# Fewer, larger transfers around attention: whole weight tiles on ScalarE's queue, keys and values of both batches per transfer

## The chip, the cores and the metric

One Trainium2 chip, one core of it. The metric is the device time of one execution in microseconds, the median of the runs. A smaller time is better.

## The reference

Three layers follow one another on fp32 data. With B=2, H=8 heads, S=768, D=40:

```python
# 1. mLSTM attention, per batch and head, for t in range(S):
m_new = max(f[t] + m, i[t]);  fs = exp(f[t] + m - m_new);  is_ = exp(i[t] - m_new)
C = fs * C + is_ * outer(v[t], k[t]);  n = fs * n + is_ * k[t]
y[t] = sigmoid(o[t]) * (C @ q[t]) / max(|n . q[t]|, 1)

# 2. soft mixture of 8 experts, 4 slots each, on x = y as [1536, 320]
logits = x @ phi                                  # [1536, 32]
slot_in = softmax(logits, axis=0).T @ x           # [32, 320]
slot_out[e] = relu(slot_in[e] @ w1[e]) @ w2[e]    # w1 [8,320,1024], w2 [8,1024,320]
x = softmax(logits, axis=1) @ slot_out            # [1536, 320]

# 3. domain mixture of 4 experts
out = sum_e p[:, e] * (relu(x @ u1[e]) @ u2[e])   # u1 [4,320,1024], u2 [4,1024,320]
```

In fp32, w1 and w2 are 10.5 MB each (8 x 320 x 1024 x 4 bytes), and q, k, v and o 1.97 MB each.

## The kernel before

Attention works on chunks of 128 positions: 6 chunks c in 2 batches b make 12 steps i (b = i % 2, c = i // 2). Within a step the scores of a chunk (stage_S, matmuls of L350), its decay matrix (stage_E: matmuls L300, exponentials L303 on ScalarE), the weighted values (stage_P1, L374), the state (stage_V, L422) and the transposes of keys (stage_K, L317), queries (qT, L274) and finished rows (stage_T1, L455) are spread over the engines. The loop `for i in range(2, NT - 1)` at L797 writes out the order of steps 2 to 10 by hand, and that written order is the order on each engine (`tc.manual_schedule()`). The logits of the soft mixture, `x @ phi`, start inside the loop: first in step 6 (L475).

After the loop come the experts of layer 2 (ffn1 with w1, matmuls L1127; ffn2 with w2, L1163), then layer 3 from about 116 us (L1232, L1276, L1292).

All data comes by DMA on two queues. SP's queue issues q, k, v, o, phi, probs, w2, u1 and u2. ScalarE's own instruction stream issues w1: `load_w1` at L84, called by `act_w` (L95) behind stage_E of each step, so that a w1 issue that has to wait holds back whatever ScalarE does next. A w1 tile is [128, 5, 512] (1280 KB: two experts, half of the hidden columns). It is fetched as two transfers, rows 0:2 (512 KB) and 2:5 (768 KB), and the table NW says how many of those 16 transfers a step issues: one ahead of the loop, one in step 2, two each in steps 3 to 9.

k and v of a chunk come per batch: 128 partitions x 8 heads x 40 floats, that is 160 KB in runs of 160 bytes; so do o and the first q. They lie in 3 buffers kvb (chunk c in c % 3), and a load into one waits for the readers of the chunk that lay there before. q of later chunks comes in pieces of 320 KB through two buffers qb.

Each DMA takes the next of 8 completion semaphores in turn, in the order in which the program issues DMAs on both queues. Before it is issued it waits until the DMA that took this semaphore last, 8 DMAs earlier, has landed. In the listings of instruction order below this is `[waits DMAHWn]`.

The lines that matter below: L88 (the w1 issue on ScalarE), L666 (stage gates2, exponentials EL and ER for chunks 4 and 5, in step 6), L684 (tokC, which empties the PSUM bank that L455 of step 6 then fills), L331 (sigmoid of o), L202, L209, L224 (loads of k, v, o), L103 (w2).

Of the kernel before, what the change touches and what calls it, by code (L numbers as in the profile page):

```python
# [8 lines left out]
F32 = mybir.dt.float32  # L9
# [6 lines left out]
NBIG = 11  # L16
NW3 = 5
NW = (1, 1, 2, 2, 2, 2, 2, 2, 2, 0)
WN = (2, 4, 2, 4)
# [3 lines left out]
def tile_mlstm_soft_moe_domain_moe(  # L23
# [16 lines left out]
    nc = tc.nc  # L40
    B, H, S, D = q.shape
# [17 lines left out]
    def bc(i):  # L59
        return i % B, i // B  # L60
# [4 lines left out]
    def slot(shape, name, dt=F32):  # L65
        return big.tile(shape, dt, tag="w", name=name)
# [16 lines left out]

    def load_w1(n, r0, r1):  # L84
        half, j = divmod(n, 4)
        if r0 == 0:
            w1s[half, j] = slot([128, 5, FH], f"w1_{n}")
        nc.scalar.dma_start(  # L88
            out=w1s[half, j][:, r0:r1],
            in_=w1[2 * j:2 * j + 2, :, half * FH:half * FH + FH].rearrange("e (p r) f -> (e p) r f", r=5)[:, r0:r1],  # L90
        )

    w1q = [(n, r0, r1) for n in range(8) for r0, r1 in ((0, 2), (2, 5))]

    def act_w(k=1):  # L95
        for _ in range(k):
            if w1q:
                load_w1(*w1q.pop(0))

    def load_w2(e, u, get):  # L100
        if u == 0:
            w2s[e] = get([128, 2, R2, DM], f"w2_{e}")
        nc.sync.dma_start(out=w2s[e][:, u], in_=w2[e, u * FH:(u + 1) * FH].rearrange("(p r) d -> p r d", r=R2))  # L103
# [13 lines left out]
    wq = [(e, u) for e in (0, 2, 4, 6) for u in range(2)]  # L117
    wq += [(e, u) for e0 in (1, 5) for u in range(2) for e in (e0, e0 + 2)]

# [6 lines left out]
    with tc.manual_schedule():  # L126
# [10 lines left out]
        with ExitStack() as actx:  # L137
# [83 lines left out]

            def load_o(i):
                b, c = bc(i)
                nc.sync.dma_start(  # L224
                    out=x1[b][:, c, 0:DM].rearrange("p (h d) -> p h d", d=D),
                    in_=o_gate[b, :, c * L:(c + 1) * L, :].rearrange("h p d -> p h d"),
                )

# [324 lines left out]

            os = list(range(NT))

            def load_os(n=1):
                for _ in range(n):
                    if os:
                        load_o(os.pop(0))

            nc.scalar.dma_start(out=gin[:, 1], in_=i_gate.rearrange("b h s -> (b h) s"))
# [18 lines left out]

# [437 lines left out]
        with mctx:  # L1018
# [368 lines left out]
```

## Time and profile before

| what | value |
| --- | --- |
| median of 3 runs | 325.69 us (325.62, 325.69, 328.19) |
| profiled execution, its own time | 323.16 us |
| its span, first to last instruction | 321.1 us |
| mean granted TensorE clock | 0.983 |
| TensorE busy (matmul) | 307.5 us, 96% of the span |
| VectorE, ScalarE, GpSimd busy | 167.2, 117.8, 92.6 us |
| DMA | 43.47 MB in 65133 packets, 49424 of them under 512 B |

The profiled execution is 2.53 us below the median of the runs, and 2.06 us of its time lie outside the span. TensorE's row in the page has one weak stretch: of its 40 slices (8.03 us each) the sixth is at 2 tenths. The clock row shows 6 and 7 tenths in the sixth to eighth slices and 9 elsewhere. The DMA row is at 8 or 9 up to the ninth slice, falls to 4, and is at 9 again up to the fourteenth. From about 121 us to the end TensorE works on layer 3 without a gap worth naming.

### The profile page before, as it was taken

The numbers are of one execution on the slowest core, as the hardware profiler recorded it, in microseconds if no ns is written. First come the engines' busy times: TensorE is split into PE (matmuls) and PEld (weight loads), VectorE is DVE, ScalarE is ACT, GpSimd is POOL, SyncE is SP. The second block draws the span as 40 slices with busy tenths as digits, with TensorE's granted clock in tenths as the row PEclk, the third lists the DMA queues.
The fourth block names the chain that finished last, engine by engine and source line by source line (L and its number), as shares of the span: only waits on it lengthen the run. The fifth ranks groups of instructions, "written<-read, shape, count | busy, mean of one in ns | idle before, by whom it ended". The sixth has DMA issues, their size and how long they took to land.

```text
span 321.1 us, 6916 instructions
## 1 busy us (share of the span) xinstructions
PE 307.5 (96%) x2846; PEld 271.3 (84%) x2846; DVE 167.2 (52%) x351; ACT 117.8 (37%) x259; POOL 92.6 (29%) x148
## 2 busy tenths in 40 slices
PE   8999992999999999999999999999999999999995
PEld 8878882888763448899999998999998999999995
DVE  6898993469536134564444444444444444444411
ACT  3868853666321034332222233333322222222200
POOL 8647772457422057900005600003800000000000
PEclk9999996699999999999999999999999999999999
DMA  7999999984999994129000001370001100011111
GB/s 138 197 188 307 306 290 211 291 235 166 353 416 415 352 302 131 24 65 306 2 3 0 0 2 33 100 262 2 0 0 27 41 2 0 22 41 41 43 61 41
DMA packets 65133, 43.47 MB, mean 135 GB/s; under 512 B 49424, under 2 KB 56624, under 8 KB 65104
## 3 DMA queue, kind: packets, MB, share of 16 engines
q1 hardware_dynamic: 59632, 32.50, 36.7%
q10 hardware_dynamic: 5472, 10.55, 9.7%
q8 instruction: 22, 0.36, 0.5%
q14 instruction: 7, 0.06, 0.0%
HBM read 39.50 MB, written 1.97 MB: 129 GB/s over the span
## 4 chain that ended last, share of the span: by engine, by line
PE 72%; DVE 1%; ACT 1%; issue 0%; POOL 0%; ACTq 0%
PE po L1292 53%; PE pa L1276 7%; PE ph L1127 3%; PE po L1163 3%; PE pg L1232 2%; PE kvp L990 1%; PE s L997 1%; PE pt L1035 1%; PE pt L1120 0%; PE pt L1090 0%; PE pt L1176 0%; DVE x L441 0%; PE po L1263 0%; PE pt L455 0%; POOL x L447 0%
## 5 line engine op out<-in xcount | busy, mean ns | idle before, releaser
L1292 PE MATMUL po<-uh,hh 128*128 128x320 f32 x768 | 170.3, 309 | 0.6 <-ACT hh L1281 0.6
L1292 PEld LDWEIGHTS po<-uh,hh 128*128 128x128 f32 x768 | 131.7, 188 | 5.8 <-POOL ul L1219 1.0
L1292 PE MATMUL po<-ul,hh 128*128 128x320 f32 x384 | 118.2, 309 | 0.0
L1282 DVE SCALAR_TENSOR_TENSOR hh<-pa,hh 128x512 fp32r<-128x512 f32 x96 | 65.8, 691 | 95.5 <-ACT hh L1281 95.5
L1281 ACT ACTIVATE hh<-pa 128x512 fp32r<-128x512 f32 x96 | 56.7, 599 | 121.7 <-PE pa L1276 120.5
L1292 PEld LDWEIGHTS po<-ul,hh 128*128 128x128 f32 x384 | 72.0, 188 | 0.0
L1217 POOL TENSOR_SCALAR uh<-u 128x640 fp32r<-128x640 f32 x16 | 11.6, 727 | 90.6 <-PE po L1292 76.3
L1276 PE MATMUL pa<-cS,gs 128*128 128x512 f32 x96 | 37.0, 397 | 0.2 <-ACT gs L1270 0.2
L1219 POOL TENSOR_TENSOR ul<-u,uh 128x640 fp32r<-128x640 f32 x16 | 25.1, 1569 | 1.3
L1300 DVE SCALAR_TENSOR_TENSOR acc<-po,pr,acc 128x320 f32<-128x320 f32 x36 | 19.6, 543 | 10.6 <-PE po L1292 10.6
L1276 PEld LDWEIGHTS pa<-cS,gs 128*128 128x128 f32 x96 | 17.9, 188 | 1.2 <-issue 0.4
L309 POOL TENSOR_SCALAR_AFFINE_SELECT w<-w 128x512 f32<-128x512 f32 x24 | 14.8, 641 | 6.4 <-ACT w L303 6.4
L356 DVE TENSOR_TENSOR w<-w,pss 128x512 f32<-128x512 f32 x24 | 15.4, 681 | 2.2 <-PE pss L350 2.0
L303 ACT ACTIVATE w<-pt 128x512 f32<-128x512 f32 x24 | 13.0, 595 | 5.6 <-PE pt L300 3.2
L350 PE MATMUL pss<-qT,kT 64*128 64x128 f32 x192 | 15.0, 299 | 0.0
L350 PEld LDWEIGHTS pss<-qT,kT 64*128 64x128 f32 x192 | 12.6, 198 | 1.8 <-issue 0.6
L447 POOL TENSOR_TENSOR x<-x,rd 128x320 f32<-128x320 f32 x11 | 8.8, 798 | 15.2 <-DVE rd L404 15.2
L455 PE MATMUL pt<-ident,x 128*128 128x128 f32 x36 | 6.5, 295 | 6.7 <-issue 6.1
L374 PE MATMUL p<-kvb,w 128*64 128x64 f32 x320 | 11.7, 230 | 0.0
L374 PEld LDWEIGHTS p<-kvb,w 128*64 128x64 f32 x320 | 11.0, 146 | 0.2 <-issue 0.2
L455 PEld LDWEIGHTS pt<-ident,x 128*128 128x128 f32 x36 | 4.1, 147 | 8.0 <-issue 6.6
L1163 PE MATMUL po<-w,hT 128*32 128x320 f32 x128 | 9.2, 434 | 0.0
(250 smaller groups left out, 316.4 us busy)
## 6 DMA issues: line engine op xcount, KB each, us to landing
w<-in_moe_w_dram SPq DMA_DIRECT2D x16, 640.0 KB, 9.1
w<-in_moe_w_dram ACTq DMA_DIRECT2D x8, 768.0 KB, 6.5
w<-in_moe_w_dram ACTq DMA_DIRECT2D x8, 512.0 KB, 4.5
u1a<-in_moe_w_dram SPq DMA_DIRECT2D x4, 1024.0 KB, 8.9
u<-in_moe_w_dram SPq DMA_DIRECT2D x3, 1280.0 KB, 10.6
kvb<-in_k_dram SPq DMA_DIRECT2D x12, 160.0 KB, 4.5
kvb<-in_v_dram SPq DMA_DIRECT2D x12, 160.0 KB, 5.3
x<-in_o_gate_dram SPq DMA_DIRECT2D x12, 160.0 KB, 4.9
```

The lines of the kernel that those rows point to most:

```text
L303: nc.scalar.activation(out=w.rearrange("p g t -> p (g t)"), in_=pt, func=AF.Exp)
L309: nc.gpsimd.affine_select(out=w, in_=w, compare_op=ALU.is_ge, fill=0.0, base=0, pattern=[[0, HP], [1, L]], channel_multiplier=-1)
L350: nc.tensor.matmul(out=pss[j][:, g, :], lhsT=kT[i][64 * j:64 * j + 64, g, :], rhs=q_of(i)[64 * j:64 * j + 64, g, :], start=True, stop=True)
L356: nc.vector.tensor_tensor(out=w, in0=w, in1=pS.pop((i, j)), op=ALU.mult)
L374: nc.tensor.matmul(out=p1[64 * x:64 * x + 64, h, :], lhsT=W[i, h % 2][:, h // 2, 64 * x:64 * x + 64], rhs=vb(i)[:, h, :], start=True, stop ...
L1163: nc.tensor.matmul(out=pos[hf][32 * j:32 * j + 32, 0:DM], lhsT=hT[:, r, 32 * j:32 * j + 32], rhs=w2s[2 * j + hf][:, r // R2, r % R2, :], s ...
L1219: nc.gpsimd.tensor_tensor(out=lo[:, r0:r0 + 2], in0=raw[:, r0:r0 + 2], in1=hi[:, r0:r0 + 2].bitcast(F32), op=ALU.subtract)
L1276: nc.tensor.matmul(out=pa, lhsT=GS[e][0][:, ft * 128:(ft + 1) * 128], rhs=cS[:, tg * 512:(tg + 1) * 512], start=True, stop=True)
L1281: nc.scalar.activation(out=hi, in_=pa, func=AF.Relu)
L1282: nc.vector.scalar_tensor_tensor(out=lo, in0=pa, scalar=0.0, in1=hi.bitcast(F32), op0=ALU.max, op1=ALU.subtract)
L1292: nc.tensor.matmul(out=po[:, 0:DM], lhsT=x[:, sl], rhs=y[e][:, ft, :], start=(ft == 0 and n == 0), stop=(ft == FT - 1 and n == 2))
L1300: nc.vector.scalar_tensor_tensor(out=dst, in0=po[:, 0:DM], scalar=pr[:, i, e:e + 1], in1=dst, op0=ALU.mult, op1=ALU.add)
```

## The change

- w1 goes as 8 transfers of 1280 KB in place of 16. The new table issues one behind stage_E of steps 2, 4, 6, 7, 8, 9 and 10, and the last behind the loop.
- k (from chunk 1 on) and v go as one transfer of 320 KB for both batches, 128 partitions x 16 x 40, so 11 transfers in place of 22. Where they stand in the program is set by a new table SPQ, together with o (four at a time, both batches of two chunks), q and phi. phi moves from step 3 to step 5, behind q7.
- Ahead of the loop SP issues what the list `k1 q2 v0 o0 q3 o1 v1 k2 q4 v2 q5` says.
- Two of the three kvb buffers, now called kw, belong to the pool that stays, with the q buffer behind each; w2 of experts 0 and 2 is loaded into them from step 9 on, half by half. The order of w2 becomes 0, 2, 4, 6, 7, 1, then 3 and 5 by halves, and NW3 (buffers of a later pool) becomes 3.

```diff
-NW3 = 5
-NW = (1, 1, 2, 2, 2, 2, 2, 2, 2, 0)
+NW3 = 3
+SPQ = {2: "k3 o2", 3: "v3 o3", 4: "k4 q6", 5: "v4 q7 p", 6: "k5 o4", 7: "o5", 8: "v5", 9: "d w"}
+NW = {2: 1, 4: 1, 6: 1, 7: 1, 8: 1, 9: 1, 10: 1}
...
-    def load_w1(n, r0, r1):
+    def load_w1(n):
         half, j = divmod(n, 4)
-        if r0 == 0:
-            w1s[half, j] = slot([128, 5, FH], f"w1_{n}")
+        w1s[half, j] = slot([128, 5, FH], f"w1_{n}")
         nc.scalar.dma_start(
-            out=w1s[half, j][:, r0:r1],
-            in_=w1[2 * j:2 * j + 2, :, half * FH:half * FH + FH].rearrange("e (p r) f -> (e p) r f", r=5)[:, r0:r1],
+            out=w1s[half, j],
+            in_=w1[2 * j:2 * j + 2, :, half * FH:half * FH + FH].rearrange("e (p r) f -> (e p) r f", r=5),
         )
...
     wq = [(e, u) for e in (0, 2, 4, 6) for u in range(2)]
-    wq += [(e, u) for e0 in (1, 5) for u in range(2) for e in (e0, e0 + 2)]
+    wq += [(e, u) for e in (7, 1) for u in range(2)]
+    wq += [(e, u) for u in range(2) for e in (3, 5)]
...
-            kvb = [ap.tile([128, 2, B, H, 64], F32, name=f"kvb{i}") for i in range(NB)]
+            KVN = 2 * B * H * 64
+            kw = [tp.tile([128, KVN + 2 * DM], F32, name=f"kw{i}") for i in range(2)]
+            kvb = [t[:, 0:KVN].rearrange("p (x b h d) -> p x b h d", x=2, b=B, h=H) for t in kw]
+            kvb.append(ap.tile([128, 2, B, H, 64], F32, name="kvb2"))
+            qw = [t[:, KVN:].rearrange("p (h x) -> p h x", h=H) for t in kw]
+            for e in (0, 2):
+                w2s[e] = kw[e // 2][:, 0:2 * R2 * DM].rearrange("p (u r d) -> p u r d", u=2, r=R2)
...
-            def load_v(i):
-                b, c = bc(i)
+            def load_kv(x, c):
+                src = (k, v)[x]
                 nc.sync.dma_start(
-                    out=vb(i)[:, :, 0:D],
-                    in_=v[b, :, c * L:(c + 1) * L, :].rearrange("h p d -> p h d"),
+                    out=kvb[c % NB][:, x].rearrange("p b h d -> p (b h) d")[:, :, 0:D],
+                    in_=src[:, :, c * L:(c + 1) * L, :].rearrange("b h p d -> p (b h) d"),
                 )
...
-            load_k(2)
-            load_q(2)
-            load_v(0)
-            load_os()
-            load_v(1)
-            load_k(3)
-            load_q(3)
-            load_os()
-            load_v(2)
-            load_q(4)
-            load_v(3)
+            load_set("k1 q2 v0 o0 q3 o1 v1 k2 q4 v2 q5")
...
-            load_k(4)
-            load_os()
-            act_w(NW[0])
-            load_q(5)
             stage_Wk(2)
             stage_T2(1)
...
                 stage_S(i)
-                if i + 3 < NT:
-                    load_k(i + 3)
-                if i in (4, 5):
-                    load_q(i + 2)
-                load_os(2 if i in (5, 6) else 1)
-                if i + 2 < NT:
-                    load_v(i + 2)
-                if i == 3:
-                    nc.sync.dma_start(out=phi_sb[:, 0:2, :], in_=phi[0:256].rearrange("(k p) n -> p k n", p=128))
-                    nc.sync.dma_start(out=phi_sb[0:64, 2, :], in_=phi[256:320])
+                load_set(SPQ.get(i, ""))
                 stage_W(i, 0)
                 stage_E(i + 1)
-                act_w(NW[i - 1])
+                act_w(NW.get(i, 0))
                 stage_P2(i)
...
             stage_T2(iL)
+            load_w(2)
+            act_w()
             stage_P1(iL - 1, "kv")
...
-            load_w(8, slot3)
+            load_w(6, slot3)
```

Before, ScalarE in step 6: w are the exponentials of the decay matrix, EL and ER those of the gates, x1_1 rows of o.

```order
L460 ACTIVATE xT_844<-pt_827 128x384 [waits PE_49]
L303 ACTIVATE w_863<-pt_861 128x512 [waits PE_49]
L303 ACTIVATE w_867<-pt_865 128x512 [waits PE_49]
L88 DMA w1_4_869<-in_moe_w1_dram 128x2x512 [waits DMAHW6_49,Pool_49]
L88 DMA w1_4_869<-in_moe_w1_dram 128x3x512 [waits DMAHW1_49]
L666 ACTIVATE EL_90<-gt2_95,gs0_92 128x256 [waits DVE_49]
```

The last DMAs on these two semaphores are the k load of chunk 4, batch 1 (DMAHW6) and the second o load (DMAHW1) of the listing of SP below. After the change, the same place:

```order
L486 ACTIVATE xT_826<-pt_809 128x384 [waits PE_49]
L329 ACTIVATE w_844<-pt_842 128x512 [waits PE_49]
L329 ACTIVATE w_848<-pt_846 128x512 [waits PE_49]
L88 DMA w1_2_850<-in_moe_w1_dram 128x5x512 [waits DMAHW0_49]
L675 ACTIVATE EL_90<-gt2_95,gs0_92 128x256 [waits DVE_49]
```

One issue stands where two stood, and its semaphore was last taken by q7, the load of kw1 from q in the second listing of SP below. Before, SP's queue in steps 5 and 6 (kvb are keys and values, x1 the o gate):

```order
L209 DMA kvb0_85<-in_v_dram 128x8x40 [waits DMAHW4_49,PE_49]
L202 DMA kvb1_86<-in_k_dram 128x8x40 [waits DMAHW6_49,PE_49,Pool_49]
L224 DMA x1_0_97<-in_o_gate_dram 128x8x40 [waits DMAHW7_49]
L224 DMA x1_1_98<-in_o_gate_dram 128x8x40 [waits DMAHW1_49]
L209 DMA kvb1_86<-in_v_dram 128x8x40 [waits DMAHW2_49,PE_49]
L202 DMA kvb2_87<-in_k_dram 128x8x40 [waits DMAHW3_49,Pool_49]
```

After the change, SP's queue in steps 4 to 6:

```order
L216 DMA kw1_86<-in_k_dram 128x16x40 [waits DMAHW4_49,PE_49,Pool_49]
L204 DMA kw0_85<-in_q_dram 128x8x80 [waits DMAHW5_49,Activation_49]
L216 DMA kw1_86<-in_v_dram 128x16x40 [waits DMAHW7_49,DMAHW0_49,PE_49]
L204 DMA kw1_86<-in_q_dram 128x8x80 [waits DMAHW0_49,Activation_49]
L239 DMA phi_sb_64<-in_moe_phi_dram 128x2x32 [waits DMAHW1_49]
L240 DMA phi_sb_64<-in_moe_phi_dram 64x32 [waits DMAHW2_49]
L216 DMA kvb2_87<-in_k_dram 128x16x40 [waits DMAHW3_49,Pool_49]
```

q7 itself waits on DMAHW0, which the first w1 tile took, and phi now stands right behind it; before, phi stood in step 3. Behind the loop SP's queue holds, after the change, w2 of experts 0 and 2 in kw:

```order
L102 DMA kw0_85<-in_moe_w2_dram 128x1280 [waits DMAHW5_49,PE_49,Pool_49]
L102 DMA kw0_85<-in_moe_w2_dram 128x1280 [waits DMAHW7_49,PE_49,Activation_49]
L102 DMA kw1_86<-in_moe_w2_dram 128x1280 [waits DMAHW1_49,PE_49,Pool_49]
L102 DMA kw1_86<-in_moe_w2_dram 128x1280 [waits DMAHW0_49,DMAHW3_49,PE_49,Activation_49]
L102 DMA w2_4_1487<-in_moe_w2_dram 128x1280 [waits DVE_49,DMAHW5_49,PE_49,Activation_49]
```

Before, the same place of SP's queue reads:

```order
L103 DMA w2_0_1506<-in_moe_w2_dram 128x1280 [waits DMAHW4_49,PE_49,Activation_49]
L103 DMA w2_0_1506<-in_moe_w2_dram 128x1280 [waits DMAHW5_49]
L103 DMA w2_2_1509<-in_moe_w2_dram 128x1280 [waits DMAHW6_49,DVE_49,Pool_49]
L103 DMA w2_2_1509<-in_moe_w2_dram 128x1280 [waits DMAHW7_49]
L103 DMA w2_4_1512<-in_moe_w2_dram 128x1280 [waits DMAHW2_49,DMAHW3_49,DMAHW0_49,PE_49]
```

There the first of them was issued at 79.61 us, in step 11. Now the halves of w2_0 wait for the last readers of chunk 3 (steps 6 and 7), and those of w2_2 for the last readers of chunk 4 (steps 8 and 9). The order of the instructions on TensorE (1113 rows) and VectorE (265 rows) is the same in both kernels.

## Rows read from the trace of the kernel before

**Rows 1.** The page: rows of TensorE and its clock, 40 slices.

```profile
PE   8999992999999999999999999999999999999995
...
PEclk9999996699999999999999999999999999999999
```

**Rows 2.** Windows, of steps 2, 6, 7 and 9, then of layer 2's ffn.

```profile
core 0: us, PE busy (x) PEld busy (x) DVE busy (x) ACT busy (x) POOL busy (x), PEclk, DMA share, GB/s
18.51:26.41 7.90, 7.11 (x116) 5.67 (x115) 6.38 (x15) 4.29 (x13) 4.16 (x7) 1.00 1.06 226
...
43.17:55.74 12.57, 6.51 (x119) 5.46 (x118) 6.60 (x18) 5.15 (x16) 5.55 (x8) 0.81 1.01 252
55.74:63.87 8.13, 8.13 (x100) 7.12 (x99) 3.99 (x11) 4.69 (x13) 3.33 (x5) 0.67 1.13 289
...
70.11:74.70 4.59, 4.59 (x90) 4.01 (x90) 3.86 (x12) 2.77 (x8) 2.63 (x4) 1.00 0.45 135
...
94.60:104.50 9.90, 9.90 (x91) 3.30 (x94) 5.58 (x18) 1.35 (x4) 2.08 (x2) 1.00 1.02 415
```

**Rows 3.** Timeline of TensorE: start, us, engine, line, operation, count, idle before it.

```profile
16.08 1.15 PE L374 MATMUL p<-kvb,w 128*64 128x64 f32 x32
...
23.59 0.66 PE L274 MATMUL pt<-ident,qb 128*128 128x128 f32 x4 [0.79 <-ACT w L303]
...
43.17 1.16 PE L350 MATMUL pss<-qT,kT 64*128 64x128 f32 x16
...
46.24 0.62 PE L422 MATMUL kv<-kvb,wkb 128*64 128x41 f32 x16
...
47.16 0.86 PE L475 MATMUL pt<-xT,phi_sb 128*32 128x128 f32 x24
...
54.67 0.87 PE L455 MATMUL pt<-ident,x 128*128 128x128 f32 x3 [6.06 <-issue]
...
55.74 2.08 PE L350 MATMUL pss<-qT,kT 64*128 64x128 f32 x16
...
61.23 0.61 PE L422 MATMUL kv<-kvb,wkb 128*64 128x41 f32 x16
```

**Rows 4.** Timeline of ScalarE in steps 2 and 6; ACTq are its DMA issues.

```profile
20.12 0.46 ACT L331 ACTIVATE x<-x 128x320 f32<-128x320 f32 x1
22.43 0.46 ACTq L88 DMA_DIRECT2D w<-in_moe_w_dram  x1
22.93 1.08 ACT L303 ACTIVATE w<-pt 128x512 f32<-128x512 f32 x2 [2.35 <-PE pt L317]
...
34.73 0.90 ACTq L88 DMA_DIRECT2D w<-in_moe_w_dram  x2
...
46.05 1.08 ACT L303 ACTIVATE w<-pt 128x512 f32<-128x512 f32 x2
51.12 2.15 ACTq L88 DMA_DIRECT2D w<-in_moe_w_dram  x2
53.31 0.60 ACT L666 ACTIVATE EL<-gt,gs 128x256 fp32r<-128x256 f32 x1 [6.18 <-DMA x<-in_o_gate_dram]
```

**Rows 5.** Timeline of SP's queue: start and length of single issues.

```profile
31.78 3.87 SPq L209 DMA_DIRECT2D kvb<-in_v_dram  x1
...
44.10 4.37 SPq L202 DMA_DIRECT2D kvb<-in_k_dram  x1
```

**Rows 6.** DMA issues of SP starting at 3.91, 17.83, 44.10 and 100.40: KB, us to landing.

```profile
kvb<-in_k_dram SPq DMA_DIRECT2D x1, 160.0 KB, 3.8
...
kvb<-in_k_dram SPq DMA_DIRECT2D x1, 160.0 KB, 3.6
...
kvb<-in_k_dram SPq DMA_DIRECT2D x1, 160.0 KB, 6.9
...
w<-in_moe_w_dram SPq DMA_DIRECT2D x1, 640.0 KB, 9.0
```

**Rows 7.** Timeline of TensorE: the second batch of ffn2 matmuls.

```profile
107.41 5.59 PE L1163 MATMUL po<-w,hT 128*32 128x320 f32 x80
```

More of the change, by code (lines that the diff above doesn't have):

```diff
@@ L82, in tile_mlstm_soft_moe_domain_moe @@
     u2s = {}
-    def load_w1(n, r0, r1):
+    def load_w1(n):
         half, j = divmod(n, 4)
-        if r0 == 0:
-            w1s[half, j] = slot([128, 5, FH], f"w1_{n}")
+        w1s[half, j] = slot([128, 5, FH], f"w1_{n}")
         nc.scalar.dma_start(
-            out=w1s[half, j][:, r0:r1],
-            in_=w1[2 * j:2 * j + 2, :, half * FH:half * FH + FH].rearrange("e (p r) f -> (e p) r f", r=5)[:, r0:r1],
+            out=w1s[half, j],
+            in_=w1[2 * j:2 * j + 2, :, half * FH:half * FH + FH].rearrange("e (p r) f -> (e p) r f", r=5),
         )
-    w1q = [(n, r0, r1) for n in range(8) for r0, r1 in ((0, 2), (2, 5))]
+    w1q = list(range(8))
     def act_w(k=1):
         for _ in range(k):
-            if w1q:
-                load_w1(*w1q.pop(0))
+            load_w1(w1q.pop(0))
     def load_w2(e, u, get):
-        if u == 0:
+        if u == 0 and e not in w2s:
             w2s[e] = get([128, 2, R2, DM], f"w2_{e}")
@@ L142, in tile_mlstm_soft_moe_domain_moe @@
             NB = 3
-            kvb = [ap.tile([128, 2, B, H, 64], F32, name=f"kvb{i}") for i in range(NB)]
+            OP = 0
+            KVN = 2 * B * H * 64
[5 more added lines that the diff above has]
+                w2s[e] = kw[e // 2][:, 0:2 * R2 * DM].rearrange("p (u r d) -> p u r d", u=2, r=R2)
             wkb = [ap.tile([128, H, 64], F32, name=f"wkb{i}") for i in range(2)]
@@ L195, in load_q @@
                 else:
-                    qb[n] = ap.tile([128, H, 2 * D], F32, tag="qb", bufs=2, name="qb")
+                    qb[n] = qw[n % 2]
                     nc.sync.dma_start(out=qb[n].rearrange("p h x -> p (h x)")[:, 0:H * r * D].rearrange("p (h x) -> p h x", h=H),
@@ L220, in x1_of, with load_o, load_phi, load_probs @@
                 return x1[b][:, c]
[L222 to L227, printed above, removed]
+            def load_o(n):
+                c, b = divmod(n, B)
+                for x in (2 * c, 2 * c + 1) if not OP else (2 * c,):
+                    y = x + 1 + OP
+                    nc.sync.dma_start(
+                        out=x1[b][:, x:y, 0:DM].rearrange("p c (h d) -> p c h d", d=D),
+                        in_=o_gate[b, :, x * L:y * L, :].rearrange("h (c p) d -> p c h d", p=L),
+                    )
+            def load_phi():
+                nc.sync.dma_start(out=phi_sb[:, 0:2, :], in_=phi[0:256].rearrange("(k p) n -> p k n", p=128))
+                nc.sync.dma_start(out=phi_sb[0:64, 2, :], in_=phi[256:320])
+            def load_probs():
+                for b in range(B):
+                    nc.sync.dma_start(out=pr[:, b::B, :], in_=probs[b * S:(b + 1) * S].rearrange("(c p) e -> p c e", p=128))
+            def load_set(names):
+                for x in names.split():
+                    if x[0] in "kv":
+                        load_kv("kv".index(x[0]), int(x[1:]))
+                    elif x[0] in "oq":
+                        (load_o if x[0] == "o" else load_q)(int(x[1:]))
+                    else:
+                        {"p": load_phi, "d": load_probs, "w": lambda: load_w(2)}[x]()
             for n in range(4):
@@ L552, in fill @@
                     nc.tensor.matmul(out=FB[:, 0:128], lhsT=x, rhs=x, start=True, stop=True)
[L554 to L559, printed above, removed]
             nc.scalar.dma_start(out=gin[:, 1], in_=i_gate.rearrange("b h s -> (b h) s"))
@@ L1025, in slot3 @@
                 return mp.tile(shape, dt, tag="w3", bufs=NW3, name=name)
-            for b in range(B):
-                nc.sync.dma_start(out=pr[:, b::B, :], in_=probs[b * S:(b + 1) * S].rearrange("(c p) e -> p c e", p=128))
-            load_w(8, slot3)
+            load_w(6, slot3)
             cps = {}
```

## The prediction

> **What bounds the kernel now.** I read the page first, then a window for each step, then the timelines of the engines in the weak step, and last the DMA issues. In the page TensorE's row is at 9 tenths almost everywhere, so the kernel is bound by TensorE, and only a hole in that row can be won by moving loads [rows 1]. There is one large hole, in the sixth slice, and the granted clock is down in the same slices. The windows put it in step 6: 12.57 us long with 6.51 us of matmuls at a mean clock of 0.81; step 7 behind it is busy all its 8.13 us, but at 0.67 [rows 2]. TensorE's timeline shows it as one gap: idle 6.06 us ahead of L455 at 54.67 [rows 3]. The profile names no releaser for it, so I followed the data: L455 needs the PSUM bank that tokC on ScalarE empties, and tokC stands behind EL (L666). ScalarE ends its exponentials at 47.13 (46.05 + 1.08), and then its w1 issues take until 53.27; EL waits 6.18 us [rows 4]. The two issues of w1_4 wait for the k load of chunk 4 (issued at 44.10, landed 6.9 us later, at 51.0 [rows 5, 6]) and for the o load behind it. So the hole is a weight load, needed 40 us later, that sits in ScalarE's stream ahead of urgent work.
>
> A smaller hole of the same kind is in step 2: the first w1 issue goes out at 22.43, the exponentials follow at 22.93, and TensorE idles 0.79 us for them [rows 3, 4].
>
> **The change, term by term** (against the profiled execution of 323.16 us, which lies 2.53 below the median).
>
> *Step 6, the idle time.* Of 16 issues 8 remain, one here, and it waits for q7. If q7 has landed when ScalarE comes to it, the issue costs what an issue that waits for nothing costs: 0.46 in step 2, 0.90 for two in step 4 [rows 4]; I take 0.4. When does q7 land? A 160 KB transfer takes 0.86 us of the queue: from the k load of 3.91 (landing 3.8 later) to that of 17.83 (landing 3.6 later) there are 16 such units, in 13.7 us [rows 6]. A w1 tile is 1280 KB, 3.16 us at the 415 GB/s of the ffn window [rows 2]. Queued up to q5 are 24 units, so q5 lands at about 3.9 + 23 x 0.86 = 23.8. Behind it, up to q7, come 16 units and 2 w1 tiles, 20.1 us: 43.9. Between the landings of the k loads of 17.83 and 44.10, 17 units and 4 w1 tiles (27.3 us by these prices) took 29.6 us, 92%; by that q7 lands at 45.7, and phi, behind it in SP's queue, at 45.9. ScalarE wants its issue at 47.13 - 0.8 = 46.3, and TensorE wants phi for L475 at 47.16 - 0.8 = 46.4 [rows 3] (0.8 is step 2's gain). That just fits. Bounds of the wait: 0, and about 1.3 us if the queue runs at 86%. I take 0.2. Gain: 6.06 - 0.4 - 0.2 = 5.5 us.
>
> *Step 7, the clock.* From the start of L350 to that of L422 step 6 takes 3.07 us (43.17 to 46.24) and step 7, with the same matmuls, 5.49 (55.74 to 61.23) [rows 3]. L350 alone takes 2.08 in place of 1.16. So 2.4 us are lost at half clock, behind an idle stretch of 6 us. Step 9, with no idle time ahead of it, runs at 1.00 [rows 2]. Without the hole I expect 1.00 throughout: gain 2.4. If half a hole stays, this gain can be nothing.
>
> *Step 2.* No w1 issue stands ahead of the exponentials any more; the one of this step comes behind them. Gain 0.8; at most the 1.85 us that the issue held ScalarE (22.43 less 20.58, where the row before it ended [rows 4]), if all of it were passed on.
>
> *The queue's issues.* SP makes 11 issues fewer and ScalarE 8. None of them lay on TensorE's path except those above; I put them at 0. What hides them is the queue, which is full in steps 2 to 7 (DMA share 1.01 to 1.13 [rows 2]). Bytes and run lengths stay the same, so the merged k and v transfers move no faster. They land later than the first half did before. The first that is needed, v0, ends with unit 9, at 10.8 by the same prices, and its matmuls L374 start at 16.08 [rows 3].
>
> *What is late next.* Two w1 tiles fewer are loaded ahead of step 6, so they must be made up later. DMA was half idle in step 9 (0.45 [rows 2]), and early w2 fills this. All work from the start is 48 units (41.3), 8 w1 tiles (25.3), 16 halves of w2 (25.3) and 0.6 of phi and probs; with 92% for the first two it ends at 3.1 + 72.4 + 25.9 = 101.4. Before, the last w2 landed at 109.4 (100.40 + 9.0 [rows 6]). The second batch of ffn2, at 107.41 before [rows 7], would start at 98.7; the third transfer from the last lands at 98.2, and the last is needed some 4 us later than the start. This fits by half a microsecond, and caps a larger gain: I put it at 0.
>
> Sum: 5.5 + 2.4 + 0.8 = 8.7. The forecast is 325.69 - 8.7 = **317.0 us** by the median (314.5 by a profile like that of before).
>
> **The rivals.**
>
> *The wait returns at the same place.* q7 and phi are now one behind the other on the path of both engines in step 6, and the k, v and o loads in front of them must wait for their buffers' readers. If they land 3 us late, at 49, TensorE idles some 2.7 us and the clock may fall again: the gain is 8.7 - 2.7 - 2.4 = 3.6, so 322; at 6 us late it is nothing. Against: by the rate of before the margin is 0.5 us, and the buffers' readers (step 4) end 10 us before the landing. For: issues in the full queue took up to 6.9 us to land [rows 6]. Chance 0.12.
>
> *The weights of ffn2 come late.* If the queue runs at 88% and w2 ends 3 us later, ffn2 waits 2 to 4 us: 319 to 321, say 320. Chance 0.10.
>
> *Slower: ScalarE's issue is held while SP issues.* SP's issue of a 160 KB load took up to 4.37 us [rows 5]. If an issue of ScalarE had to wait until SP's is finished, and a merged one takes twice as long, one such hold is up to 8.7 us. In step 6 that is more than the hold of before: from a hold of about 7 us on there (6.06 of idle time and 0.8 of step 2) nothing is gained. One of 8.7 leaves 8.7 - 0.8 = 7.9 us on TensorE in place of 6.06, and the lost clock remains: 325.7 + 1.8 - 0.8 = 326.7; a second one, in step 7 or 8, would make about 334. Against: ScalarE's two issues at 34.73 took 0.90 us together in the middle of SP's issue of 31.78 to 35.65 [rows 4, 5]. Chance 0.06. [...]
>
> That the change doesn't do what it says is excluded by the order: one issue stands ahead of EL where two stood.
>
> **How the numbers follow.** The forecast has 0.72. Its own range: the most is 5.7 + 2.4 + 1.85 = 9.95, the least, with 1.3 us of wait and 1.5 of the clock, 6.1, so 315.7 to 319.6. The profiled execution lay 2.53 below the median, and the runs of the changed kernel may lie on its level, so the low end goes to 313.2, rounded to 313.0. The high end takes in late weights and the larger part of the returned wait: 322.5. A change of 1% is 3.3 us, which is about what can be told from no change. Faster by over 1% (below 322.4): the forecast, late weights, and a little of the returned wait: 0.72 + 0.10 + 0.02 = 0.84. Within 1%: the rest of the returned wait and the single hold, 0.10 + 0.01 = 0.11. Slower by over 1%: the repeated hold, 0.05.
>
> **What would show it.** Right: L475, L317 and the L455 matmuls of step 6 follow one another with under 1 us idle; the clock is 1.00 in all slices to the ninth; ScalarE's issue in step 6 takes about 0.4 us and EL starts within 1 us of the exponentials' end; step 7 takes about 5.8 us; q7 and phi land at 45 to 46.5; ffn2 runs without a wait for w2. Wrong: an idle stretch ahead of L475 or of the step's L455 with a landing of q7 or phi behind 48; a wait of ffn2 for a transfer; or an issue of ScalarE of several us with its semaphore long free, which would be the held issue.

## The result, and the profile after

The changed kernel takes 317.95 us (median of 4 runs, 316.79 to 319.12) against 326.94 before (4 runs): ratio 0.972, 95% interval 0.964 to 0.980. The forecast was 317.0. Profiled, it took 317.03 with a span of 315.3, where the kernel before had 323.16 and 321.1. Between the two profiles lie 6.1 us, between the medians 9.0, since the profile of before, at 323.16, was shorter than any of those four runs (325.62 to 328.93). Executions of one kernel differ by up to 2.4% (the kernel before, beside e10 below: 321.41 to 329.04 us), so medians here are of all runs, while ratios compare only those within 1.5% of a kernel's fastest. Of the runs so compared beside e10 below, those of the kernel before with a granted clock of 0.982 to 0.989 took 321.4 to 324.3 us, those with 0.973 to 0.979 took 325.4 to 325.7. There, with more runs, the same change comes to 0.982 (0.974 to 0.990), about 6 us, near the difference of the two profiles; the medians lie 8.4 apart.

The page of the changed kernel, TensorE and clock, to be held against [rows 1]:

```profile
PE   8899979999999989999999999999999999999995
...
PEclk9999995999999999999999999999999999999999
```

Counted from the first, the weak slice of [rows 1] is the seventh (48.2 to 56.2 us), with the clock at 6 tenths in the seventh and eighth; the text ahead says the sixth. That hole is gone, but in the seventh slice the clock still stands at 5 tenths. The windows of steps 2, 6, 7 and 9, and the stretch up to ffn2 (columns as in [rows 2]), show where:

```profile
17.22:24.23 7.01, 6.95 (x116) 5.72 (x115) 6.83 (x17) 4.74 (x14) 4.77 (x8) 1.00 0.99 235
...
40.75:49.47 8.72, 6.49 (x118) 5.39 (x117) 6.38 (x18) 5.06 (x16) 5.55 (x8) 0.95 0.87 173
49.47:57.88 8.41, 8.41 (x101) 7.40 (x100) 4.09 (x11) 4.78 (x13) 3.33 (x5) 0.65 1.13 317
...
64.11:68.70 4.59, 4.59 (x90) 4.01 (x89) 3.85 (x12) 2.77 (x8) 2.63 (x4) 1.00 1.06 377
...
88.59:98.47 9.88, 9.88 (x88) 3.28 (x91) 5.58 (x18) 1.35 (x4) 2.08 (x2) 1.00 1.01 397
```

Step 2 is 0.89 shorter than in [rows 2], step 6 3.85 shorter, step 7 0.28 longer: it still runs at a mean clock of 0.65. DMA is busy in step 9 (1.06 against 0.45). TensorE's timeline through step 6:

```profile
44.37 0.44 PE L684 MATMUL pt<-ident,gt 128*128 128x128 f32 x2
46.80 0.86 PE L501 MATMUL pt<-xT,phi_sb 128*32 128x128 f32 x24 [2.00 <-DMA phi_sb<-in_moe_phi_dram]
...
48.49 0.79 PE L481 MATMUL pt<-ident,x 128*128 128x128 f32 x3 [0.23 <-issue]
...
49.47 2.08 PE L376 MATMUL pss<-qT,kT 64*128 64x128 f32 x16
```

The 6.06 us ahead of L455 [rows 3] have become 2.00 us ahead of the phi matmuls (L501, before L475) and 0.23 behind them. ScalarE waits at the same time, for q7, as its timeline shows:

```profile
43.62 1.07 ACT L329 ACTIVATE w<-pt 128x512 f32<-128x512 f32 x2
46.54 0.55 ACTq L88 DMA_DIRECT2D w<-in_moe_w_dram  x1
47.13 0.60 ACT L675 ACTIVATE EL<-gt,gs 128x256 fp32r<-128x256 f32 x1 [2.44 <-DMA kw<-in_q_dram]
```

Both transfers land within 0.3 us of each other: q7, issued at 41.33, after 5.2 us (46.5), and phi, issued at 42.91, after 3.8 us (46.7, and its second part at about 46.8).

### The profile page after: what moved, and what is told of

The parts are those of the page before. It is cut to its first block, busy times and chain, and to the rows that moved or that the text cites. A ratio compares the mean times of both kernels' runs of the same rounds, so it can differ in the third digit from the quotient of the medians.

```text
span 315.3 us, 6899 instructions
## 1 busy us (share of the span) xinstructions
PE 305.0 (97%) x2846; PEld 268.8 (85%) x2846; DVE 167.3 (53%) x351; ACT 117.6 (37%) x259; POOL 92.9 (29%) x148
## 4 chain that ended last, share of the span: by engine, by line
PE 73%; DVE 1%; ACT 1%; issue 1%; POOL 0%; POOLq 0%
PE po L1288 54%; PE pa L1272 7%; PE ph L1123 3%; PE po L1159 3%; PE pg L1228 2%; PE kvp L988 1%; PE s L995 1%; PE pt L1031 1%; PE pt L1116 0%; PE pt L1086 0%; PE pt L1172 0%; DVE x L467 0%; PE pt L481 0%; PE po L1259 0%; POOL x L473 0%
## 5 line engine op out<-in xcount | busy, mean ns | idle before, releaser
L1288 PE MATMUL po<-uh,hh 128*128 128x320 f32 x768 | 170.3, 309 | 0.5 <-ACT hh L1277 0.5
L1288 PEld LDWEIGHTS po<-uh,hh 128*128 128x128 f32 x768 | 131.7, 188 | 5.8 <-POOL ul L1215 0.9
L1288 PE MATMUL po<-ul,hh 128*128 128x320 f32 x384 | 118.2, 309 | 0.0
L1288 PEld LDWEIGHTS po<-ul,hh 128*128 128x128 f32 x384 | 72.0, 188 | 0.0
L376 PE MATMUL pss<-qT,kT 64*128 64x128 f32 x192 | 15.0, 299 | 0.0
L376 PEld LDWEIGHTS pss<-qT,kT 64*128 64x128 f32 x192 | 12.6, 198 | 1.9 <-ACT qT L314 0.6
L400 PE MATMUL p<-kw,w 128*64 128x64 f32 x256 | 9.7, 234 | 0.0
L1123 PE MATMUL ph<-w,lhs 128*32 128x512 f32 x80 | 9.2, 596 | 0.0
L400 PEld LDWEIGHTS p<-kw,w 128*64 128x64 f32 x256 | 9.0, 149 | 0.2 <-issue 0.2
L392 PEld LDWEIGHTS p<-gs,qT 128*64 128x64 f32 x160 | 6.7, 145 | 2.5 <-issue 2.2
(259 smaller groups left out, 316.1 us busy)
```

Source lines behind the costliest of these rows:

```text
L376: nc.tensor.matmul(out=pss[j][:, g, :], lhsT=kT[i][64 * j:64 * j + 64, g, :], rhs=q_of(i)[64 * j:64 * j + 64, g, :], start=True, stop=True)
L400: nc.tensor.matmul(out=p1[64 * x:64 * x + 64, h, :], lhsT=W[i, h % 2][:, h // 2, 64 * x:64 * x + 64], rhs=vb(i)[:, h, :], start=True, stop ...
L1123: nc.tensor.matmul(out=ph[32 * j:32 * j + 32, :], lhsT=lhs1[:, r, j, :], rhs=w1s[u, j][:, r, :], start=(r == 0), stop=(r == 4))
L1288: nc.tensor.matmul(out=po[:, 0:DM], lhsT=x[:, sl], rhs=y[e][:, ft, :], start=(ft == 0 and n == 0), stop=(ft == FT - 1 and n == 2))
```

## Experiments

Each kernel ran beside the kernel before, which gives its ratio. Since the start of step 2 lies between 17.2 and 18.9 us from profile to profile, also for one and the same kernel (17.22 and 18.33 for the changed one), I compare two stretches of each profile: from step 2 to step 11 (starts of the score matmuls, attention) and from there to the first L1292 of layer 3 (L1288 after the change; it holds ffn1 and ffn2). The column "last w2" is the landing of the last w2 transfer.

| kernel | attention | ffn1, ffn2 | sum | last w2 | ratio to before (interval) |
| --- | --- | --- | --- | --- | --- |
| before | 59.84 | 42.85 | 102.69 | 109.4 | 1 |
| after | 55.13 | 42.74 | 97.87 | 103.4 | 0.972 (0.964 to 0.980) |
| e1 | 62.83 | 42.84 | 105.67 | 111.8 | 1.002 (0.998 to 1.006) |
| e2 | 52.50 | 45.50 | 98.00 | 106.5 | 0.983 (0.977 to 0.988) |
| e3 | 55.78 | 43.54 | 99.32 | 106.1 | 0.986 (0.980 to 0.993) |
| e5 | 50.68 | 49.20 | 99.88 | 106.4 | 0.981 (0.976 to 0.986) |
| e6 | 50.61 | 44.59 | 95.20 | 103.6 | 0.976 (0.972 to 0.981) |
| e7 | 55.31 | 44.60 | 99.91 | 107.6 | 0.980 (0.974 to 0.986) |
| e8 | 60.30 | 42.75 | 103.05 | 110.9 | 0.982 (0.975 to 0.989) |
| e9 | 58.60 | 42.75 | 101.35 | 108.0 | 0.982 (0.976 to 0.987) |
| e10 (after again) | 53.19 | 44.09 | 97.28 | 105.4 | 0.982 (0.974 to 0.990) |
| e11 | 58.06 | 42.76 | 100.82 | 106.7 | 0.993 (0.987 to 0.998) |
| e12 | 55.36 | 42.73 | 98.09 | 98.2 | 0.981 (0.975 to 0.986) |
| e13 | 59.38 | 42.77 | 102.15 | 101.5 | 1.004 (0.998 to 1.010) |

**e1: the kernel before without the w1 issues of step 6.**

```diff
-NW = (1, 1, 2, 2, 2, 2, 2, 2, 2, 0)
+NW = (1, 1, 2, 2, 2, 0, 2, 2, 2, 2)
```

> The kernel before, with one thing changed: the two w1 transfers of step 6 are left out there and issued in step 10. Theory (the hole of step 6 is the w1 issue ahead of EL, and the half clock of step 7 follows from the hole): the idle stretch ahead of L455 falls from 6.06 us to under 0.6, step 7 takes about 5.8 us in place of 8.13, the profile comes to about 323.2 - 5.8 - 2.3 = 315.1, ratio about 0.975; a late w2 may give 1 to 2 us back. Rival (the whole set of transfers has to be rearranged; the k and o loads are late for ScalarE or TensorE by themselves): an idle stretch of 3 us or more stays in step 6, ratio 0.99 or above.

The median was 325.93 against 325.67: no change, where 0.975 was expected. Step 6 healed (idle 0.66 us), but the hole moved. First ScalarE, then TensorE in step 7:

```profile
58.87 1.06 ACTq L88 DMA_DIRECT2D w<-in_moe_w_dram  x2
59.97 0.74 ACT L254 ACTIVATE qx<-qb 128x640 f32<-128x640 f32 x1 [3.82 <-DMA kvb<-in_v_dram]
```

```profile
23.29 0.66 PE L274 MATMUL pt<-ident,qb 128*128 128x128 f32 x4 [1.07 <-ACT w L303]
...
25.51 1.85 PE L612 MATMUL pt<-gs,gt 16*128 16x256 f32 x4 [0.39 <-ACT kT L322]
27.29 2.08 PE L350 MATMUL pss<-qT,kT 64*128 64x128 f32 x16
...
60.76 1.97 PE L274 MATMUL pt<-ident,qx 128*128 128x128 f32 x8 [3.33 <-ACT qx L254]
63.30 2.08 PE L350 MATMUL pss<-qT,kT 64*128 64x128 f32 x16
```

In step 7 the same two issues now stand ahead of qx and wait for an o and a v load, 8 transfers back each; the v load (issued at 54.60) lands at about 59.3. So the hole is not tied to EL: the w1 issue in ScalarE's stream made it in step 7 as it had in step 6. It does not do so everywhere: the issues of steps 3 to 5 (0.37 to 0.90 us long) left no hole on TensorE. The lines up to 27.29 are code that e1 shares with the kernel before. Here the holes of step 2 were a little longer than the 0.79 of [rows 3], and step 3 ran at half clock (0.50 from 27 to 31 us; 8.78 us from L350 to L350). Such a second stretch may be what its longer runs have; no trace of one was taken.

**e2, e3, e5: the two waits of step 6, one by one.** e2 has phi early, and ScalarE's issue no longer takes q7's semaphore; e3 takes only ScalarE's issue away from EL; e5 has phi early but keeps ScalarE's wait for q7.

```diff
# e2
-SPQ = {2: "k3 o2", 3: "v3 o3", 4: "k4 q6", 5: "v4 q7 p", 6: "k5 o4", 7: "o5", 8: "v5", 9: "d w"}
+SPQ = {2: "k3 o2", 3: "v3 o3 p", 4: "k4 q6", 5: "v4 q7", 6: "k5 o4", 7: "o5", 8: "v5", 9: "d w"}
# e3
-                act_w(NW.get(i, 0))
+                act_w(NW.get(i, 0) if i != 6 else 0)
...
+                if i == 6:          # behind tokC
+                    act_w(NW[i])
# e5
+SPQ = {2: "k3 o2", 3: "v3 o3 p", 4: "k4 q6", 5: "v4 q7 d", 6: "k5 o4", 7: "o5", 8: "v5", 9: "w"}
```

> The changed kernel, with phi issued in step 3 (behind o3) in place of step 5 (behind q7). With two DMAs fewer between them, ScalarE's w1 issue of step 6 now takes the semaphore of the w1 tile before it and no longer that of q7, so both waits of step 6 (TensorE for phi, ScalarE for q7) are gone. Theory (either wait alone makes the hole of 2.2 us, and the half clock of step 7 follows from it): no idle stretch over 0.6 us in step 6, clock 1.00 in step 7, profile about 317.0 - 2.0 - 2.4 = 312.6. Rival A (the half clock in step 7 does not come from so short a gap): profile about 315, clock still near 0.65 in step 7. Rival B (the next late transfer takes over: w2 lands at 103.4 and ffn2, earlier by 4 us, waits for it): step 6 and 7 heal, ffn2 waits 1 to 3 us, profile 314 to 316.

> The changed kernel, with ScalarE's w1 issue of step 6 moved behind tokC, so that it no longer stands ahead of EL; phi stays late. Theory (two waits side by side, each enough): TensorE's idle stretch ahead of the phi matmuls stays at about 2.0 us, the clock of step 7 stays near 0.65, profile within 0.7 us of 317.0. Rival (ScalarE's issue is the wait that counts, phi is hidden): profile 312 to 315.

> The changed kernel, with phi in step 3 and the two transfers of probs in phi's old place behind q7, so that ScalarE's w1 issue of step 6 still takes q7's semaphore and waits for it, while TensorE's phi is early. Theory (two waits side by side): the idle stretch of about 2 us moves to L481 behind ScalarE's EL and tokC, the clock of step 7 stays near 0.65, profile within 0.7 us of 317.0. Rival (phi is the wait that counts and ScalarE's issue is hidden behind it): profile 312 to 315.

e3 went as the theory said at its place: TensorE idled 3.05 us for phi, which landed at about 48, step 7 began at half clock (its first L376 took 2.03 us in place of 1.16), nothing was won. Its profile (318.35) lies 1.3 us above the changed kernel's, where 0.7 was allowed. e2 healed step 6 (0.67 us) and ran at clock 1.00 to the end, 2.6 us less in attention. It kept a hole of 1.84 us in step 7, behind ScalarE's next w1 issue, and it gave 2.8 back behind attention: rival B, with w1 as the late transfer in place of w2. Its profile (318.80) missed the range of every theory; 1.65 us of that are a later start of step 2 (18.87).

e5's own profile did not show the expected hole: q7 landed at 46.3 and held ScalarE only 0.5 us past the end of its exponentials (45.81), TensorE idled 0.94, and step 7 took 5.72 us at full clock. But the wait for q7 is not refuted by it. e7 and e12 below have the same code in attention, with phi early and the wait for q7 kept. In them q7 landed at 47.7 and 47.3, ScalarE was held 2.1 us, TensorE idled 2.55 and 2.54, and half clock followed (0.50 from 51 to 55 us in both). So either wait alone can make the hole, phi's in e3 and q7's in e7 and e12, and when the loads land decides whether it does. ScalarE in e5, then in e12:

```profile
44.73 1.08 ACT L329 ACTIVATE w<-pt 128x512 f32<-128x512 f32 x2
46.28 0.55 ACTq L88 DMA_DIRECT2D w<-in_moe_w_dram  x1
```

```profile
44.19 1.08 ACT L330 ACTIVATE w<-pt 128x512 f32<-128x512 f32 x2
47.33 0.56 ACTq L88 DMA_DIRECT2D w<-in_moe_w_dram  x1
47.93 0.60 ACT L676 ACTIVATE EL<-gt,gs 128x256 fp32r<-128x256 f32 x1 [2.66 <-DVE gs L461]
```

e5 won 4.5 us in attention against the profile above (2.5 against e10's). All of it, and 2.0 more, was lost behind it: 3.73 us in one wait, and about 1.7 in the half clock after it (mean 0.59 from 95 to 99 us; 18 matmuls of L1123 in 4.46 us, where e2 has 2.76). This profile is also the longest of e5's six runs (320.16; their median is 317.64). TensorE in e2, then in e5:

```profile
55.50 1.15 PE L300 MATMUL pt<-ident,qx 128*128 128x128 f32 x8 [1.84 <-ACT qx L280]
56.91 1.20 PE L376 MATMUL pss<-qT,kT 64*128 64x128 f32 x16
...
95.12 2.76 PE L1123 MATMUL ph<-w,lhs 128*32 128x512 f32 x18 [1.71 <-DMA w<-in_moe_w_dram]
```

```profile
48.23 0.52 PE L481 MATMUL pt<-ident,x 128*128 128x128 f32 x3 [0.94 <-POOL ER L677]
...
94.78 4.46 PE L1123 MATMUL ph<-w,lhs 128*32 128x512 f32 x18 [3.73 <-DMA w<-in_moe_w_dram]
```

The transfer waited for is the last w1 tile, and its issue shows 19.0 us to landing in the changed kernel and 25.3 in e5. The first fence is the changed kernel, the second e5: the packets of both queues from 84 to 91 us (q1 is SP's, with w2; q10 ScalarE's, with w1), then the issue of the tile at 69.46:

```profile
w<-in_moe_w_dram ACTq DMA_DIRECT2D x1, 1280.0 KB, 19.0
```

```profile
q1 hardware_dynamic: 428, 1.95, 69.2%
q10 hardware_dynamic: 429, 0.88, 33.2%
...
w<-in_moe_w_dram ACTq DMA_DIRECT2D x1, 1280.0 KB, 25.3
```

428 against 429 packets: here each queue gets as many as the other. w2's packets are larger (4.6 KB against 2.1 on average), so w2, needed later, gets 69% of the bytes and the last w1 tile 31%.

**e6 and e7: the last w1 tile and w2.** Both start from e5.

```diff
# e6
-        nc.scalar.dma_start(
+        (nc.sync if n == 7 else nc.scalar).dma_start(
# e7: SPQ[9] = "", and behind the loop
+            for t in kw:
+                nc.gpsimd.memset(t[:, 0:8], 0.0)
-            load_w(2)
+            load_w(4)
```

> The kernel of e5 (probs in phi's old place), with the last w1 tile issued on SP's queue, behind w2 of expert 2 and ahead of all other w2, in place of ScalarE's queue. Theory (with the attention part healed, the last w1 tile is what bounds: on ScalarE's queue it gets every second packet, 2 KB against w2's 5 KB, and took 25.3 us from issue to landing in e5, so that L1123 waits 3.7 us for it): it lands before 88 us, the wait of L1123 falls from 3.7 us to under 0.5, w2 still ends by about 105, and the span is 4 to 6 us shorter than e5's profile (318.4): 312.5 to 314.5, median near 314. Rival (the DMA queue as a whole is the bound; what w1 gains, w2 loses): ffn2 waits 3 us or more for w2, the span stays above 316.

> The kernel of e5, with w2 of experts 0 and 2 held back until step 11 (two memsets of 8 columns on GpSimd ahead of their loads), so that no w2 shares the queue with the w1 tiles of steps 8 to 10. This undoes the early w2 of the change. Theory (w2 takes the bandwidth of the last w1 tiles): the last w1 tile lands before 85 us and L1123 doesn't wait; w2 ends 0 to 3 us later than in e5 (106.4), so ffn2 waits up to 3 us; span 313 to 316. Rival (early w2 is what keeps the DMA queue full, without it the total ends later): w2 ends behind 110 us, ffn2 waits over 4 us, span 317 or more.

In e6 the tile landed at 84.5, ffn1 did not wait, and the span was 314.2, the shortest profile of all. What was left is a wait for w2:

```profile
87.83 5.36 PE L1123 MATMUL ph<-w,lhs 128*32 128x512 f32 x48
...
100.35 2.08 PE L1159 MATMUL po<-w,hT 128*32 128x320 f32 x26 [0.86 <-DMA w<-in_moe_w_dram]
```

The median was 317.97, not the 314 expected: five of its six runs had a granted clock of 0.988 to 0.993, so by their mean clock some half clock came back in them. The profile of e12, whose attention is the same code, shows such a run (below). e7's tile landed at 85.1, no wait of ffn1; w2 ended at 107.6, within the range given, ffn2 waited 1.1, and the attention part fell into the hole (2.55 us, then half clock). The span of 318.0 met the rival's number, though not by its landing behind 110.

**e8, e9, e10, e11: the size of the transfers.** e8 has w1 by halves again, e9 k and v per batch, e11 both; e10 is the changed kernel.

```diff
# e8, e11
+        for r0, r1 in ((0, 2), (2, 5)):
+            nc.scalar.dma_start(
+                out=w1s[half, j][:, r0:r1],
...
# e9, e11
+                for b in range(B):
+                    nc.sync.dma_start(
+                        out=kvb[c % NB][:, x, b][:, :, 0:D],
+                        in_=src[b, :, c * L:(c + 1) * L, :].rearrange("h p d -> p h d"),
...
```

> The changed kernel, with each w1 tile again as two transfers (rows 0:2 and 2:5) issued back to back where the whole tile was issued: only the number of transfers is undone. Theory (the gain comes from when the loads are issued, not from their number): the same as the changed kernel within 1%, the hole in step 6 2 to 3 us long, since the second half waits for phi's semaphore. Rival (twice the issues on ScalarE and twice the semaphores bring the long holds back): holds of ScalarE of 4 us or more, 1% to 2% slower than the changed kernel, ratio above 0.985.

> The changed kernel, with k and v again as one transfer per batch, two issues in a row at the places of the new order: only the merging is undone. Theory (the bytes and the run length of 160 bytes are the same, so the queue is no slower): the same as the changed kernel within 1%. Rival (fewer, larger transfers are themselves faster, or 11 more issues on SP delay q7 and phi): phi lands 1 us or more later than 46.8, hole in step 6 of 3 us or more, ratio above 0.985.

> The changed kernel once more, as it is, so that the three others can be compared with it on the same chip. Expected: ratio 0.970 to 0.982; a span in its profile of 211 to 212 us behind the landing of the last w2 transfer (in the first profile 103.4 and 315.3), since that sum has been 210.4 to 212.0 in every profile so far.

> The changed kernel with both size changes undone (w1 by two transfers per tile, k and v per batch); what stays is the new order, the later phi, fewer w1 tiles ahead of step 6, and the early w2. Theory A (order and early w2 bring the gain, the size of a transfer brings nothing): within 1% of the changed kernel of this job, last w2 at 103 to 105. Theory B (each transfer waits for the one 8 transfers before it, so smaller transfers keep fewer bytes in flight and hold ScalarE and SP more often; e8 and e9 point that way): 1% to 2% slower than the changed kernel of this job, last w2 at 108 to 111, holds of ScalarE ahead of qx in step 7 of 2.5 us or more.

e10 and e11 ran on one chip, in one job: medians of 317.93 and 321.57. By their ratios e11 gains 0.7%, about 2.4 us, and e10 1.8%, about 6.0. So whole tiles and merged k and v bring some 3.6 us of the 6; the two intervals overlap a little (up to 0.990 and from 0.987), so the sizes' share is likely, not certain. Either size alone is not shown to cost anything: e8 and e9, in another job, have ratios of 0.982 like e10, under the 0.985 of their rivals. The holes of step 6 are about those of the changed kernel (1.98 and 0.66 us in e8, 2.17 and 0.55 in e9), though phi landed later in e9, at about 49. What is new are the holds of theory B: ahead of qx in step 7 in e9, and in e8, whose profile is its longest run (3.72 us on TensorE); in e11 in step 2, and only 1.04 us in step 7. First e9, then ScalarE and TensorE in e11:

```profile
58.71 1.97 PE L301 MATMUL pt<-ident,qx 128*128 128x128 f32 x8 [2.64 <-ACT qx L281]
```

```profile
23.86 2.41 ACTq L89 DMA_DIRECT2D w<-in_moe_w_dram  x2
26.32 0.60 ACT L350 ACTIVATE kT<-pt 128x512 f32<-128x512 f32 x1 [5.90 <-DMA kw<-in_q_dram]
```

```profile
26.97 1.13 PE L623 MATMUL pt<-gs,gt 16*128 16x256 f32 x4 [3.70 <-ACT kT L350]
28.02 1.98 PE L378 MATMUL pss<-qT,kT 64*128 64x128 f32 x16
```

A second issue for the same tile is a second semaphore to wait for; that the 8 transfers in flight then hold fewer bytes is my reading, not shown. Against theory B, e11's last w2 landed at 106.7, not 108 to 111. In e10 the span lies 210.4 us behind that landing, under the 211 to 212 expected; e12 and e13, with 217.9 and 218.7, show that this difference is no constant.

**e12, e13: less w2.** e6 and the kernel before, each with four w2 transfers left out.

```diff
# e12 (e6)
-    wq += [(e, u) for u in range(2) for e in (3, 5)]
...
+            if e in (1, 7):
+                w2s[{1: 3, 7: 5}[e]] = w2s[e]
# e13 (before)
-    wq += [(e, u) for e0 in (1, 5) for u in range(2) for e in (e0, e0 + 2)]
+    wq += [(e, u) for e0 in (1,) for u in range(2) for e in (e0, e0 + 2)]
...
+            if e in (1, 3):
+                w2s[e + 4] = w2s[e]
```

> The kernel of e6 with the w2 transfers of experts 3 and 5 left out (these experts use the tiles of experts 1 and 7 in their place), 2.6 MB or 6.3 us of the queue less. Theory (in e6 the queue still bounds, but TensorE's own work lies only about 2 us under it): the wait of ffn2 for w2 goes, the span falls by 1 to 2.5 us to 311.7 to 313.2, and no more, though the queue ends 6 us earlier. Rival (the queue bounds alone): the span falls by 5 us or more. Second rival (TensorE bounds already): within 0.5 us of e6.

> The kernel before with four w2 transfers left out (experts 5 and 7 use the tiles of experts 1 and 3), again 6.3 us of the queue less. Theory (the kernel before is bound by TensorE and the holes of steps 6 and 7; w2 lands about 1 us ahead of need): within 0.5% of the kernel before. Rival (the landing of w2 bounds the kernel before as well): 5 us or more faster, ratio 0.985 or less.

e13 took 325.62 against 326.29, ratio 1.004: the kernel before was not bound by the landing of its weights, though the last landed 7.9 us earlier. e12's median is 317.49, e6's 317.97 in another job. Its span of 316.1 missed the expectation, since its attention fell into the hole:

```profile
49.28 0.81 PE L482 MATMUL pt<-ident,x 128*128 128x128 f32 x3 [2.54 <-issue]
50.29 2.08 PE L377 MATMUL pss<-qT,kT 64*128 64x128 f32 x16
```

Behind attention it took 42.73 us in place of e6's 44.59. But its attention ended 3.7 us later than e6's (step 11 at 73.16 against 69.43), and the changed kernel, with step 11 at 72.35 and all of w2, took 42.74. So e12 does not show what less w2 would give, and the theory stays open.

## Why the prediction was right, point by point

The total was right, the sum only in part: of its three terms one came as forecast, one in part, and one, in the profile, not at all. Of the signs set down for being right, the one on ffn2 held, and q7 came at the edge of its range; the hole, the clock, EL's start and step 7 were off.

*What bounded the kernel before*: right. e13 takes 6.3 us of loads away and moves nothing; the holes in attention set the time. e1 adds that the w1 issue makes them, and that moved out of step 6 it made one in step 7.

*Step 2, 0.8*: 0.89 by the profiles. In e1 the holes of step 2 are followed by a step at half clock; there steps 2 and 3 took 18.13 us, after the change 13.41, so the term was worth up to 4.7 in such a run, which the forecast left out.

*Step 6, 5.5*: 3.85. The failed step is the 0.2 us for q7 and phi. The runs showed 2.23 us in its place (2.00 and 0.23). q7 and phi landed at 46.5 and 46.8, against 45.7 and 45.9 forecast. In this profile the larger part is the other side: TensorE came at 44.8, not at 46.4. It was 1.3 us early from the start of step 2 and gained 0.9 there and 0.2 in steps 3 to 5, while the loads did not come earlier with it. The early start is no part of the change, and it is not the whole cause. e10, the same kernel, started step 2 at 18.33, TensorE came at 45.9, and phi's matmuls began only at 47.7:

```profile
47.68 0.86 PE L501 MATMUL pt<-xT,phi_sb 128*32 128x128 f32 x24 [1.77 <-DMA phi_sb<-in_moe_phi_dram]
```

There the landing, 1.8 us behind the forecast, is the larger part. So the margin of half a microsecond was too small for the spread of either side; and its upper bound for the wait, 1.3, comes to about 1.0 when it is redone with 86%, less than what came.

*Step 7, 2.4*: nothing in the profile. Step 7 took 8.41 us at 0.65. This follows from the step before: the forecast of 1.00 rested on a hole of 0.2 us, with the remark that half a hole could cost the gain, and 2.00 and 0.23 us did. Where the holes stay under 1 us (e5, e6) step 7 takes 5.72, so the term exists. In the profile of e10 the hole was 1.77 us and step 7 began at full clock (1.00 from 47 to 55 us). The three other runs of the changed kernel had clocks of 0.998 to 1.000, so they lost next to nothing to half clock; yet they took 316.79 to 319.12, hardly less than the profiled run or more. e10, also at 1.000, shows where such a gain can go: attention 1.94 us shorter than in the first profile, the stretch behind it 1.35 longer, step 2 started 1.11 later.

*What stands in the place of the missing 4.2 us* (8.7 less 0.89, 3.85 and -0.28): 1.29 us by the profiles are the start, where the kernel before ran its first transposes (4 to 9 us) at about 1.1 us for four instead of 0.6. That is not the change: e10 has the long ones too, with nearly the late start of before (18.33 against 18.51). The rest lies between profile and median: the mean clocks of 0.983 in the profile of before and 0.972 in e1's come to about 11 and 18 us at half clock, and of the 23 compared runs of the kernel before beside e1 and e10, 11 lie at 0.973 to 0.979. That speaks for a second stretch at half clock in them, against one or none in the changed kernel. No trace of such a run of the kernel before itself was taken. That the total met the forecast within 1 us is in this part luck: in e10's job the compared runs give about 6 us for the same change.

*What is late next*: w2 ended at 103.4 (forecast 101.4) and ffn2 did not wait. What was late first is the last w1 tile: L1123 waits 0.31 us for it in e10, 1.71 in e2 and 3.73 in e5. The cap was seen, but at w2; the last w1 tile the forecast had not followed. DMA's idle time did go into early w2: the share from 71 to 83 us is 0.52 before and 1.03 after.

*The rivals*: the wait returned at the same place, at 2.2 us and with the half clock. Late weights came as soon as attention got faster (e2, e5). That ScalarE's issue is held while SP issues did not show: its w1 issue at 59.65 took 0.55 us in the middle of an SP issue that lasted 5.86 from 54.17.

*The queue's issues, put at nothing*: not quite. e11 puts the size of the transfers at some 3.6 of the 6 us gained by the ratios of that job, with intervals that overlap.

No version clearly beat the changed kernel: e6 has the best profile and the same median.

## What to carry to other kernels

A load issued from ScalarE's stream held ScalarE here until the transfer that it must wait for, the one 8 transfers before, had landed (in step 6 EL came after 6.18 us of ScalarE's idle time before the change, after 2.44 us with it); keep such issues few, and not ahead of work that TensorE waits for. When a stall goes, shift the needs of everything behind it earlier and hold them against landings that do not move: here the profile of e5 won another 2.5 to 4.5 us in attention and lost as much or more behind it, mostly to a late tile in ffn1. Before saying what a stall costs, look at several executions: the same load landed 1.4 us apart in the same code (q7 at 46.3 in e5 and at 47.7 in e7), and a hole of about 2 us was followed by a step at half clock in one trace (2.00 us in the changed kernel) and not in another (2.17 in e9).

## What the runs showed of the hardware

- While w1 and w2 loaded side by side, the two queues got nearly equal numbers of packets in two windows: 428 (SP's) and 429 (ScalarE's) from 84 to 91 us of e5, 127 and 124 from 82 to 84 us of the changed kernel. In e5 the queue with the larger packets so got more bytes (69% against 31%). In two others the numbers were not equal: 393 against 129 from 86 to 91 us of the changed kernel, shortly ahead of the landing of the last w1 tile, and 896 of SP's queue, with loads in runs of 160 bytes, against 91 of ScalarE's in the kernel before, 28 to 29 us.
- In the changed kernel the clock fell late: TensorE idled from 44.8 to 46.8, worked at 1.00 again, with 0.23 us of idle time ahead of 48.5, and ran at 0.50 from about 48.6 until about 55.4:

```profile
47.00:48.00 1.00, 1.00 (x28) 0.80 (x20) 0.28 (x2) 0.87 (x2) 0.52 (x1) 1.00 1.30 233
48.00:49.00 1.00, 0.77 (x6) 0.56 (x5) 0.95 (x4) 1.00 (x6) 0.00 (x0) 0.80 0.76 115
49.00:50.00 1.00, 1.00 (x8) 0.94 (x8) 0.62 (x4) 0.76 (x3) 0.08 (x1) 0.50 0.97 325
...
55.00:56.00 1.00, 1.00 (x24) 0.95 (x21) 0.49 (x1) 0.00 (x0) 1.00 (x3) 0.79 0.88 239
```

  The holes of 2.54 to 3.73 us in e1, e3, e5, e7, e9, e11 and e12 were followed by half clock (the lowest window of 4 us behind them has a mean of 0.50 in e1, e7, e9 and e12, 0.59 in e5, 0.65 in e11, 0.76 in e3); those of 1.84 and 1.71 us in e2 were not (1.00). Of those between, 2.00 and 0.23 in the changed kernel were, 2.17 and 0.55 in e9 were not; and e1 had half clock behind 1.07 and 0.39. No run here shows what decides between them.
- In the first 4 to 9 us the same group of four transposes took 1.11 us in the profile of before and 0.66 in that of the changed kernel, with the granted clock at 1.00 in both. So the clock row does not tell the two starts apart.
